# A gated linear recurrence with a SwiGLU feed-forward: rotated rows moved on chip, two units of gates first, feed-forward groups of four chunks

## The chip, the core and the metric

The kernel runs on one core of a Trainium2 chip. TensorE (PE) multiplies matrices, VectorE (DVE) and ScalarE (ACT) work on elements, GpSimd (POOL) does one small operation for each chunk, and SyncE (SP) issues nearly all transfers in the order of its queue. The metric is the device time of one execution in microseconds (us). Every matmul here is in float32, and the profile shows each of them as two instructions.

## The reference

Four sequences of 768 steps, eight heads of 48 features. Each head carries a complex 48 x 48 state that decays and rotates with a gate of its own for each feature and step; the output goes through an RMS norm and a SwiGLU feed-forward of 384 to 1536 to 384.

```python
mag = np.sqrt(a_re * a_re + a_im * a_im)
scale = np.minimum(mag, 0.999) / (mag + 1e-06)
a_re_n, a_im_n = (a_re * scale, a_im * scale)
for t in range(S):
    ar, ai = (a_re_n[:, :, t, :, None], a_im_n[:, :, t, :, None])
    new_re = ar * S_re - ai * S_im
    new_im = ar * S_im + ai * S_re
    kv = np.einsum('bhd,bhe->bhde', k[:, :, t], v[:, :, t])
    S_re, S_im = (new_re + kv, new_im)
    y[:, :, t] = np.einsum('bhd,bhde->bhe', q[:, :, t], S_re)
...
xn = x / np.sqrt(np.mean(x * x, axis=-1, keepdims=True) + 1e-06) * rms_g
g = xn @ w_gate
return ((g * (1.0 / (1.0 + np.exp(-g)))) * (xn @ w_val)) @ w_out
```

## The kernel before

The 3072 rows are cut into 24 chunks of 128 steps (`C`), six to a sequence. Three pieces of work go over them with different steps.

**Gates, by units of two chunks** (`load_gates(u)` and `gates(u)`, 12 units). Features lie on the partitions, 128 at a time in three blocks j, and the 256 steps of the unit on the free axis, so each element-wise instruction is 128 x 768. Magnitudes are multiplied up within a chunk by one scan (tile `p`, L592) and angles are added up by three scans (L612). Then k is divided and q multiplied by the magnitude, and both by the sine and the cosine of the angle. These four products (L501, `rot<-k,y` and so on) go into the tile `rot`, which has a 129th column for the decay of the chunk. For the matmuls, the 96 rows of a head (48 sine and 48 cosine) must lie on the partitions, with the heads on the free axis. `rot` is therefore written to a buffer in device memory (`way`, L629) and read back in the other shape (`kq`, L631), one transfer each way for each chunk. `gates` is a generator; at each `yield` other work is emitted between its parts. Most tiles of it have one buffer: `s`, `w`, `y`, `r`, `p`, and also `k` and `q`, while `re` and `im` have two.

**Attention, by chunks** (`scores(n)` and `finish(n)`). `scores` multiplies k with q for each head (`s_ps`, L721), masks the result (`am`, L723) and transposes k (`kt_ps`, L732, copied by ACT at L733). `finish` of the chunk adds up the state (`state_ps`, L744), makes the output (`y_ps`, L755 and L757), then a chain of small steps: the square and its sum on ACT (L761), `ssq` on DVE (L762), a power on POOL (L765), the scaled copy `xn` on ACT (L767), three transposes on PE (`xT_ps`, L774), and `xT` on DVE (L775).

**Feed-forward, by groups of `GC` = 3 chunks** (`feed_forward(g)`, 8 groups). For each of 12 blocks f of 128 hidden features, six gate and six value matmul instructions run over the 384 columns of the group (L792); ACT makes the silu into `sg` (L795), and DVE multiplies it with the value into `hT`. Then `out_ps` (L803) adds up over the 12 blocks for each chunk, ACT copies it to `ot`, and SP stores it.

The weights come as eight-byte numbers in this launch, so each of 18 pieces is loaded as `raw` (L659) and narrowed to float32 by one instruction of ACT and six of DVE (`narrow`, L671 to L680).

**The order.** The main loop emits, for each n, `scores(n)` and then `finish(n-1)`. After each yield of these, one or two steps of the running feed-forward (`filler`) and one step of the next unit's gates (`ahead`) are emitted. Group g starts after `finish` of its last chunk. What is emitted is not yet the order on the engines: a planner takes the emitted order as a priority, puts an instruction onto its engine's queue as soon as its own cost estimates say that it is ready, and adds the waits. So later work can fill a gap that the planner sees. On the chip each queue then runs in its fixed order, SP's included. When a pool's buffer is taken again, the new tile waits for all readers and writers of the old one.

```python
for n in range(N + 1):
    if n % UC == 0 and n // UC + 1 < NU:
        for _ in ahead:
            pass
        if n // UC + 2 < NU:
            load_gates(n // UC + 2)
        ahead = gates(n // UC + 1)
```

Of the kernel before, what the change touches and what calls it, by code (L numbers as in the profile page):

```python
# [28 lines left out]
P = 128  # L29
# [442 lines left out]
def fast(tc, ctx, qT, kT, v, a_re, a_im, w_gate, w_val, w_out, rms_g, out, H, bad):  # L472
# [10 lines left out]
    GC = 3  # L483
# [6 lines left out]
    assert NCH % GC == 0 and NCH % UC == 0 and DM % P == 0 and D2 <= P and L * ND == D  # L490
# [23 lines left out]
    def load_gates(u):  # L514
# [15 lines left out]
        for n in range(u * UC, (u + 1) * UC):  # L530
            U[n]["v"] = unit.tile([C, H, D], FP32, tag="v", name="v", bufs=4)
            nc.sync.dma_start(out=U[n]["v"].rearrange("t h d -> t (h d)"),
                              in_=v[n * C:(n + 1) * C, :])

    rot = consts.tile([P, 4 * ND, UC, C + 1], FP32, name="rot")
    nc.vector.memset(rot[:, :, :, C:], 0.0)
    load_gates(0)

    zeros = consts.tile([P, T], FP32, name="zeros")
    nc.gpsimd.memset(zeros, 0.0)
# [17 lines left out]
    def gates(u):  # L560
# [4 lines left out]
        s, w, y, r, p = (prep.tile([P, ND, T], FP32, tag=x, name=x)  # L565
                         for x in ("s", "w", "y", "r", "p"))
# [29 lines left out]
        nc.vector.tensor_copy(  # L596
            out=rot[:, 2 * ND:, :, C].rearrange("p (a j) c -> p a j c", j=ND),
            in_=ends[:, u].unsqueeze(1).to_broadcast([P, 2, ND, UC]))
# [12 lines left out]
        for j in range(ND):  # L611
            nc.vector.tensor_tensor_scan(  # L612
                out=re[:, j], data0=im[:, j], data1=zeros, op0=ALU.add, op1=ALU.add,
# [9 lines left out]
        for i, (x, f) in enumerate(((k, y), (k, s), (q, y), (q, s))):  # L623
            tt(rot[:, i * ND:(i + 1) * ND, :, 0:C], by_chunk(x), by_chunk(f))
        yield
        for i in range(UC):
            n = u * UC + i
            way = dram.tile([4 * DM, C + 1], FP32, tag="way", name="way")
            nc.sync.dma_start(out=way.rearrange("(r p) t -> p r t", p=P), in_=rot[:, :, i])  # L629
            to = unit.tile([D2, 2, H, C + 1], FP32, tag="kq", name="kq", bufs=3)  # L630
            nc.sync.dma_start(out=to.rearrange("d x h t -> d x (h t)"),  # L631
                              in_=way.rearrange("(x d h) t -> d x (h t)", x=2, h=H))
            U[n]["k"], U[n]["q"] = to[:, 0, :, 0:C], to[:, 1, :, 0:C]
            U[n]["decay"] = to[:, 1, :, C:]
        yield
# [26 lines left out]
    def narrow(stage, to, raw):  # L662
# [5 lines left out]
        t, g = (stage.tile([P, n], I32, tag=x, name=x, bufs=1) for x in ("t", "g"))  # L668
        as_to = lambda x: x.rearrange("p (c f) -> p c f", f=cols)

        nc.scalar.activation(out=to, in_=as_to(hi.bitcast(FP32)), func=AF.Square)  # L671
        stt(as_to(g.bitcast(FP32)), to, (1.125 * 2.0 ** -15) ** 2, as_to(hi.bitcast(FP32)), ALU.is_ge)

        nc.vector.tensor_scalar(out=t, in0=g, scalar1=3, scalar2=0x3FFFFFFF,
                                op0=ALU.logical_shift_left, op1=ALU.bitwise_and)
        stt(t, g, -2 ** 30, t, ALU.bitwise_and, ALU.bitwise_or)

        nc.vector.tensor_scalar(out=g, in0=t, scalar1=-2 ** 23, scalar2=None, op0=ALU.bitwise_and)
        stt(to, as_to(lo.bitcast(U32)), 2.0 ** -52, as_to(g.bitcast(FP32)), ALU.mult)
# [32 lines left out]
    def scores(n):  # L712
# [3 lines left out]
        am = u["am"] = unit.tile([C, H, C], FP32, tag="am", name="am")  # L716
        hh = H // 2
        for a in range(2):
# [4 lines left out]
            nc.vector.tensor_tensor(out=am[:, a * hh:(a + 1) * hh], in0=ps, op=ALU.mult,  # L723
# [4 lines left out]
        kt = u["kt"] = unit.tile([C, H, D2], FP32, tag="kt", name="kt")  # L728
        for a in range(2):
# [3 lines left out]
            nc.scalar.copy(out=kt[:, a * hh:(a + 1) * hh], in_=ps)  # L733
# [97 lines left out]
    for n in range(N + 1):  # L831
# [11 lines left out]
        if n > 0:  # L843
            run(finish(n - 1), 2)
# [75 lines left out]
```

## Time and profile before

| | before |
|---|---|
| time, median of 3 runs (lowest to highest) | 891.09 us (880.48 to 893.98) |
| the profiled execution: time, span | 884.13 us, 882.3 us |
| mean granted clock of PE | 0.939 |
| busy: PE, PEld (weight loads), DVE, ACT, POOL | 773.3, 530.1, 426.8, 356.2, 23.2 us |
| gate_ps + val_ps matmuls (576 + 576 of 128x384) | 209.4 + 207.7 us |
| out_ps matmuls (576 of 128x384) | 192.8 us |
| chain that ended last: PE, DMA, DVE, ACT | 80%, 10%, 6%, 2% |
| transfers way and kq | 24 each of 774 KB, 8.9 and 5.7 us from issue to landing |
| moved in all | 81.17 MB |

The span runs from the first instruction to the last, and the execution's time lies 1.8 us above it. Mean durations of matmuls overlap, because they are pipelined: the step from one start to the next is what counts. The "chain that ended last" is followed back from the last instruction; its shares say on what the end depended. Waits are read from the engine that waits: "PE s_ps <- DMA kq" is time in which PE stood until a transfer into kq had landed.

### The profile page before, as it was taken

How to read it: one execution, taken by the hardware profiler on the slowest of the kernel's cores; microseconds unless marked ns; L12 is line 12 of the kernel's file. 1: busy time of each engine (PE TensorE's matmuls, PEld its weight loads, DVE VectorE, ACT ScalarE, POOL GpSimd, SP SyncE). 2: the span in 40 equal slices, each digit the busy share in tenths (PEclk: the TensorE clock that was granted, in tenths of full speed). 3: DMA queues.
4: the chain of work that ended last, by engine and by line, in shares of the span. 5: the costliest groups of instructions: out<-in, count | busy, mean ns of one | idle time of the engine just before them, and what ended most of it. 6: DMA issues, size and time to landing. Idle time of an engine off the chain costs nothing.

```text
span 882.3 us, 8797 instructions
## 1 busy us (share of the span) xinstructions
PE 773.3 (88%) x3370; PEld 530.1 (60%) x3370; DVE 426.8 (48%) x654; ACT 356.2 (40%) x520; POOL 23.2 (3%) x42
## 2 busy tenths in 40 slices
PE   0051879888879999999999999999999999999997
PEld 0051857675455566676666667666666767665554
DVE  5978768858978787768785101210121112210110
ACT  6845565643537887676783111111111111110100
POOL 1000000000000000000000000000000000000000
PEclk9995569968989999989999999999999999999999
DMA  8748374852673565482763120112111100000000
GB/s 293 154 110 201 103 169 118 202 138 72 182 186 101 114 154 156 96 189 71 137 162 73 46 63 26 29 45 55 35 29 45 43 21 1 1 9 19 1 1 30
DMA packets 85602, 81.17 MB, mean 92 GB/s; under 512 B 4144, under 2 KB 74800, under 8 KB 85552
## 3 DMA queue, kind: packets, MB, share of 16 engines
q1 hardware_dynamic: 85120, 80.13, 36.3%
q8 instruction: 28, 0.46, 0.2%
q10 hardware_dynamic: 432, 0.39, 0.1%
q14 instruction: 22, 0.18, 0.1%
HBM read 56.77 MB, written 23.74 MB: 91 GB/s over the span
## 4 chain that ended last, share of the span: by engine, by line
PE 80%; DMA 10%; DVE 6%; ACT 2%; issue 1%; SPq 1%; POOL 0%; ACTq 0%; DVEq 0%
PE val_ps L792 20%; PE gate_ps L792 20%; PE out_ps L803 19%; PE s_ps L721 6%; PE y_ps L755 5%; DMA way<-rot 4%; PE y_ps L757 4%; DMA kq<-way 4%; PE state_ps L744 3%; PE kt_ps L732 2%; DVE rot L501 1%; PE xT_ps L774 1%; DMA raw<-in_w_gate_dram 1%; DVE p L592 1%; DVE g L504 1%
## 5 line engine op out<-in xcount | busy, mean ns | idle before, releaser
L792 PE MATMUL gate_ps<-xT,wg 128*128 128x384 f32 x576 | 209.4, 501 | 5.5 <-DVE wg L501 4.8
L792 PE MATMUL val_ps<-xT,wv 128*128 128x384 f32 x576 | 207.7, 497 | 2.2 <-ACT sg L795 2.2
L803 PE MATMUL out_ps<-wo,hT 128*128 128x384 f32 x576 | 192.8, 491 | 0.2
L792 PEld LDWEIGHTS val_ps<-xT,wv 128*128 128x128 f32 x576 | 111.4, 194 | 80.1 <-issue 4.3
L501 DVE TENSOR_TENSOR hT<-val_ps,sg 128x384 f32<-128x384 f32 x96 | 53.3, 555 | 215.8 <-PE val_ps L792 200.4
L792 PEld LDWEIGHTS gate_ps<-xT,wg 128*128 128x128 f32 x576 | 109.0, 196 | 73.7 <-issue 7.9
L803 PEld LDWEIGHTS out_ps<-wo,hT 128*128 128x128 f32 x576 | 108.7, 192 | 71.7 <-issue 1.8
L721 PE MATMUL s_ps<-kq 96*128 96x128 f32 x384 | 57.2, 311 | 77.3 <-DMA kq<-way 77.3
L795 ACT ACTIVATE sg<-gate_ps 128x384 f32<-128x384 f32 x96 | 47.0, 490 | 176.6 <-PE gate_ps L792 176.2
L721 PEld LDWEIGHTS s_ps<-kq 96*128 96x128 f32 x384 | 55.5, 224 | 84.0 <-DMA kq<-way 55.6
L755 PE MATMUL y_ps<-v,am 128*128 128x48 f32 x384 | 76.0, 294 | 0.0
L757 PE MATMUL y_ps<-state,kq 96*128 96x48 f32 x320 | 68.2, 298 | 0.0
L755 PEld LDWEIGHTS y_ps<-v,am 128*128 128x128 f32 x384 | 62.9, 211 | 1.1
L723 DVE TENSOR_TENSOR am<-s_ps,causal 128x512 f32<-128x512 f32 x48 | 32.7, 688 | 51.5 <-PE s_ps L721 51.4
L761 ACT ACTIVATE x<-y_ps 128x384 f32<-128x384 f32 x24 | 11.8, 491 | 110.6 <-PE y_ps L757 101.4
L757 PEld LDWEIGHTS y_ps<-state,kq 96*128 96x128 f32 x320 | 55.1, 215 | 0.3
L808 ACT COPY ot<-out_ps 128x384 f32<-128x384 f32 x24 | 11.4, 475 | 99.3 <-PE out_ps L803 99.3
L765 POOL TENSOR_TENSOR rs<-ssq,mhalf 128x1 f32<-128x1 f32 x24 | 20.8, 867 | 754.7 <-DVE ssq L762 754.7
L733 ACT COPY kt<-kt_ps 128x384 f32<-128x384 f32 x40 | 17.6, 479 | 50.1 <-PE kt_ps L732 50.1
L744 PEld LDWEIGHTS state_ps<-v,kt 128*96 128x96 f32 x320 | 33.0, 179 | 4.4 <-issue 2.4
L744 PE MATMUL state_ps<-v,kt 128*96 128x48 f32 x320 | 32.6, 259 | 0.0
L762 DVE TENSOR_SCALAR ssq<-ssq 128x1 f32<-128x1 f32 x24 | 3.6, 152 | 58.6 <-ACT x L761 58.6
(100 smaller groups left out, 722.6 us busy)
## 6 DMA issues: line engine op xcount, KB each, us to landing
way<-rot SPq DMA_DIRECT2D x24, 774.0 KB, 8.9
kq<-way SPq DMA_DIRECT2D x24, 774.0 KB, 5.7
re<-in_a_re_dram SPq DMA_DIRECT2D x36, 128.0 KB, 2.6
k<-in_k_dram SPq DMA_DIRECT2D x24, 192.0 KB, 2.9
q<-in_q_dram SPq DMA_DIRECT2D x24, 192.0 KB, 3.3
v<-in_v_dram SPq DMA_DIRECT2D x24, 192.0 KB, 2.4
raw<-in_w_gate_dram SPq DMA_DIRECT2D x6, 768.0 KB, 8.2
raw<-in_w_val_dram SPq DMA_DIRECT2D x6, 768.0 KB, 7.0
```

Source lines behind the costliest of these rows:

```text
L501: nc.vector.tensor_tensor(out=o, in0=x, in1=y, op=op)
L721: nc.tensor.matmul(ps[:, h], lhsT=k[:, a * hh + h], rhs=q[:, a * hh + h], start=True, stop=True)
L723: nc.vector.tensor_tensor(out=am[:, a * hh:(a + 1) * hh], in0=ps, op=ALU.mult, in1=causal.unsqueeze(1).to_broadcast([C, hh, C]))
L732: nc.tensor.transpose(ps[:, h], k[:, a * hh + h], ident[0:D2, 0:D2])
L733: nc.scalar.copy(out=kt[:, a * hh:(a + 1) * hh], in_=ps)
L744: nc.tensor.matmul(ps[:, h], lhsT=u["kt"][:, h], rhs=vv[:, h], start=True, stop=True)
L755: nc.tensor.matmul(ps[:, h], lhsT=am[:, h], rhs=vv[:, h], start=True, stop=prev is None)
L757: nc.tensor.matmul(ps[:, h], lhsT=q[:, h], rhs=prev[:, h], start=False, stop=True)
L765: nc.gpsimd.tensor_tensor(out=rs, in0=ssq, in1=mhalf, op=ALU.pow)
L792: nc.tensor.matmul(p_, lhsT=w_[:, d, fs], rhs=xT[:, d], start=d == 0, stop=d == ND - 1)
L795: nc.scalar.activation(out=sg, in_=gp, func=AF.Silu)
L803: nc.tensor.matmul(ps, lhsT=hT[:, f, i * C:(i + 1) * C], rhs=wo[:, f], start=f == 0, stop=f == NF - 1)
```

## The change

- **The way on chip.** `rot`, `way` and `kq` are gone. The four products go into `ks`, `k`, `qs` and `q` themselves (the cosine products in place), and each of their three blocks is moved by one transfer from SBUF to SBUF into the unit's tiles `kr` and `qr`: 12 transfers, each from 128 partitions with a row of 1 KB to 16 partitions with eight such rows. The decays go through memory by themselves (`dec`, 8 bytes for each feature, and two reads into `de`).
- **Order.** At n = 0 all of `gates(1)` is emitted ahead of `scores(0)`; before, it was emitted in steps between the parts of chunks 0 and 1. The first three weight pieces are emitted, and the feed-forward's pool opened, at n = 2 and not at n = 3.
- **Groups of four.** `GC` is 4: six groups, gate and value matmuls over 512 columns, and group 0 starts after `finish(3)`, which follows `scores(4)`.
- **Room for it.** The silu is written straight into `hT` (no `sg`); `am` and `kt` are made of two half tiles (four and two buffers, so `kt` holds one chunk and not two); `v` has three buffers and not four; `ot` has one and not two; `x` shares `xn`; the zeros of the angle scan are one broadcast column; `narrow` works in the weight's own place with one scratch tile in two buffers.

```diff
-    GC = 3
+    GC = 4
...
-            U[n]["v"] = unit.tile([C, H, D], FP32, tag="v", name="v", bufs=4)
+            U[n]["v"] = unit.tile([C, H, D], FP32, tag="v", name="v", bufs=3)
...
-        nc.vector.tensor_copy(
-            out=rot[:, 2 * ND:, :, C].rearrange("p (a j) c -> p a j c", j=ND),
-            in_=ends[:, u].unsqueeze(1).to_broadcast([P, 2, ND, UC]))
+        dec = dram.tile([DM, UC], FP32, tag="dec", name="dec")
+        nc.sync.dma_start(out=dec.rearrange("(j p) c -> p j c", p=P), in_=ends[:, u])
+        de = unit.tile([D2, H, UC], FP32, tag="decay", name="decay", bufs=3)
+        for a in range(2):
+            nc.sync.dma_start(out=de[a * D:(a + 1) * D].rearrange("d h c -> d (h c)"),
+                              in_=dec.rearrange("(d h) c -> d (h c)", h=H))
...
-        for i, (x, f) in enumerate(((k, y), (k, s), (q, y), (q, s))):
-            tt(rot[:, i * ND:(i + 1) * ND, :, 0:C], by_chunk(x), by_chunk(f))
-        yield
+        kq = {n: unit.tile([D2, H, T], FP32, tag=n, name=n) for n in ("kr", "qr")}
+        for to, x, xs in ((kq["kr"], k, ks), (kq["qr"], q, qs)):
+            for a, (o, f) in enumerate(((xs, s), (x, y))):
+                tt(o, x, f)
+                rows = (1 - a) * D
+                for j in range(ND):
+                    nc.sync.dma_start(out=to[rows + j * L:rows + (j + 1) * L], in_=o[:, j])
+            yield
         for i in range(UC):
             n = u * UC + i
-            way = dram.tile([4 * DM, C + 1], FP32, tag="way", name="way")
-            nc.sync.dma_start(out=way.rearrange("(r p) t -> p r t", p=P), in_=rot[:, :, i])
-            to = unit.tile([D2, 2, H, C + 1], FP32, tag="kq", name="kq", bufs=3)
-            nc.sync.dma_start(out=to.rearrange("d x h t -> d x (h t)"),
-                              in_=way.rearrange("(x d h) t -> d x (h t)", x=2, h=H))
-            U[n]["k"], U[n]["q"] = to[:, 0, :, 0:C], to[:, 1, :, 0:C]
-            U[n]["decay"] = to[:, 1, :, C:]
-        yield
+            U[n]["k"], U[n]["q"] = (kq[x][:, :, i * C:(i + 1) * C] for x in ("kr", "qr"))
+            U[n]["decay"] = de[:, :, i:i + 1]
...
+            am.append(unit.tile([C, hh, C], FP32, tag="am", name="am", bufs=4))
...
+            kt.append(unit.tile([C, hh, D2], FP32, tag="kt", name="kt", bufs=2))
...
-            sg = ffn.tile([P, GT], FP32, tag="sg", name="sg")
-            nc.scalar.activation(out=sg, in_=gp, func=AF.Silu)
-            tt(hT[:, f], vp, sg)
+            nc.scalar.activation(out=hT[:, f], in_=gp, func=AF.Silu)
+            tt(hT[:, f], vp, hT[:, f])
...
-            ot = ffn.tile([C, DM], FP32, tag="ot", name="ot")
+            ot = ffn.tile([C, DM], FP32, tag="ot", name="ot", bufs=1)
...
             ahead = gates(n // UC + 1)
+            if n == 0:
+                for _ in ahead:
+                    pass
...
         if n > 0:
             run(finish(n - 1), 2)
+        if n == UC:
+            for _ in range(EARLY):
+                next(pieces)
+            first.close()
+            ffn = ctx.enter_context(tc.tile_pool(name="ffn", bufs=2))
         if n % GC == 0 and n:
             for _ in filler:
                 pass
-            if n == GC:
-                for _ in range(EARLY):
-                    next(pieces)
-                first.close()
-                ffn = ctx.enter_context(tc.tile_pool(name="ffn", bufs=2))
             filler = feed_forward(n // GC - 1, pieces, ffn)
```

## The prediction

> **What bounds the kernel now.** I read the 40 slices first, then the wait table of TensorE (PE) by stretches, then the windows, then the order of time around the stalls.
>
> The slices (digits are tenths; PEclk is the granted clock) show two kernels in one:
>
> ```profile
> PE   0051879888879999999999999999999999999997
> DVE  5978768858978787768785101210121112210110
> PEclk9995569968989999989999999999999999999999
> ```
>
> From slice 13 on PE is full at full clock while VectorE (DVE) goes idle; before, DVE is 70 to 90% busy and PE has holes and a half clock. Windows, with columns length, busy PE, PEld, DVE, ACT, POOL, clock, DMA share, GB/s:
>
> ```profile
> 49.00:123.00 74.00, 43.56 (x234) 42.34 (x234) 53.49 (x81) 38.84 (x53) 4.08 (x3) 0.61 0.53 135
> 123.00:275.00 152.00, 128.34 (x565) 89.75 (x566) 124.94 (x185) 78.86 (x108) 4.53 (x5) 0.88 0.58 145
> ...
> 400.00:780.00 380.00, 380.00 (x1753) 259.06 (x1752) 112.69 (x191) 98.88 (x173) 7.94 (x13) 1.00 0.21 51
> ```
>
> PE's waits, asked for 0 to 275 us and for the rest: the rest is empty, and the first stretch has
>
> ```profile
> PE s_ps L721 <- DMA kq<-way: 77.3, 5, 48.8
> PE xT_ps L774 <- ACT xn L767: 15.4, 6, 6.4
> PE gate_ps L792 <- DVE wg L501: 4.8, 2, 3.1
> ```
>
> So the time is: when PE becomes saturated, plus the PE work that is left then. Group 0 of the feed-forward starts at 122.9 and ends at 275.1; what follows is 882.3 - 275.1 = 607.2 us without a wait of PE. From PE's order of time:
>
> ```profile
> 86.02 3.75 PE L721 MATMUL s_ps<-kq 96*128 96x128 f32 x16 [17.28 <-DMA kq<-way]
> ...
> 122.94 3.82 PE L792 MATMUL gate_ps<-xT,wg 128*128 128x384 f32 x6 [0.65 <-DVE xT L775]
> ...
> 275.11 2.10 PE L792 MATMUL gate_ps<-xT,wg 128*128 128x384 f32 x6
> 277.05 2.10 PE L792 MATMUL val_ps<-xT,wv 128*128 128x384 f32 x6
> ```
>
> **Part 1, groups of four.** At full clock six gate matmuls of 384 columns start 1.935 us apart from the next six, so 0.3225 us each. 128-column ones (s_ps, 16 in 1.78 us) take 0.111, so a line through both gives 0.428 for 512 columns; plain proportion gives 0.430. A group of three costs 24 x 1.935 + 23.2 (72 out_ps, from 852.96 on) = 69.7 us; one of four 24 x 2.58 + 96 x 0.3225 = 92.9. Eight groups of the one are 557.6, six of the other 557.4: the PE work itself is not shortened. What changes is what is behind PE when it saturates. At the end of group 0, four chunks instead of three are through, 23.2 us more. With the same chunks 0 to 7 and chunk 8's scores done, the rest is 607.2 - 23.2 = 584.0.
>
> Group 0 is also where the weights are narrowed. One piece costs DVE 4 x 0.87 + 2 x 0.47 = 4.4 us (start to start), a pair of gate and value pieces 8.8, and the hT products of its two f-steps 0.9. PE streams those two steps in 7.7 us now and in 10.3 after: six pairs in which PE outran DVE by 2.0 us become six in which it doesn't. That is 12 us of loss.
>
> The silu written into hT saves no instruction and adds no wait: hT is freed by the last out_ps, which precedes gate_ps on PE's queue anyway. ACT and DVE get fewer, longer instructions (96 x 0.56 to 72 x about 0.7 us), hidden by PE's 2.6 us per accumulation. One ot buffer: its copy comes every 7.7 us, its store lands in 1.8. All 0; without that cover 24 x 1.8 us at most.
>
> **Part 2, two units first.** Today unit 1's products end on DVE at 70.5. Between 36.1 and 70.5, DVE waits 3.4 + 0.9 + 0.7 us for s_ps and state_ps of chunks 0 and 1, and does four masks and a state, 2.9 us. Put behind unit 1's gates, these 7.9 leave the way: 62.6. Bounds: 0 to 16 (another 8 us of narrowing lies there, which only fills gaps). If the gap filling already does all that, it is 0.
>
> **Part 3, the way on chip.** The chain that ended last shows the hop through memory, and SP's order of time the price of an issue with 1 KB rows:
>
> ```profile
> 34.88 7.19 DMA way<-rot
> 42.08 6.66 DMA kq<-way
> 48.79 3.78 PE s_ps L721 x16
> ```
> ```profile
> 27.24 1.83 SPq L522 DMA_DIRECT2D re<-in_a_re_dram  x3
> ```
>
> and the page's table of issues its landing (KB each, median us from issue):
>
> ```profile
> re<-in_a_re_dram SPq DMA_DIRECT2D x36, 128.0 KB, 2.6
> ```
>
> Removed per unit: two way and two kq transfers, 14.2 us from the last product (34.6) to s_ps (48.8). Added: 12 transfers of 128 KB from SBUF to SBUF, plus dec and two de. The nearest row is re: 128 KB in 128 rows of 1 KB, 0.61 us to issue, 2.6 to land. The first three can go when the first product is done, 2.6 us before the last: 12 x 0.61 + 2.6 - 2.6 = 7.3 us after the last product, a gain of 6.9. Bounds: 4.1 (all 1.57 MB at the 232 GB/s that the two kq made in 6.66 us, 6.7 - 2.6), and 12 x 2.6 - 2.6 = 28.6 (each waits for the one before it). I take 7.3, since re's issues do go out back to back. The four products stay (0.95 us each); two small copies give way to dec and de, whose small rows I price at gcol's 5.4 us each; they leave some ten DVE instructions before the products, so they are hidden, else up to 10.8 us.
>
> Against this speaks the Trainium skill, "SBUF — State Buffer", section "Door 1: The DMA port swizzle": a transfer reaches only the ports of its partitions, and partitions 0 to 15 get 104 GB/s. Each of these transfers writes 16 partitions; an estimate from that page is 1.26 us each and 15 us for twelve, so about 15 after the last product in place of 7.3, and a sum some 8 to 15 us longer. No row here has so few partitions.
>
> **New waits.** k and q are now read by transfers, in one buffer: the load of the next unit's k must wait for them, and behind it on SP's queue stand the later loads, v, and weight pieces; DVE waits for k in mid-gates. k's rows leave about 5 us after unit 0's products, the load lands 3 us later, and q follows 4 us on; in unit 1 q*p runs at 58.0, 23 us after those products. Covered; if not, 5 us a unit for units 1 to 4. v has three buffers: v of chunk n waits for y of n-3, a place where SP already stood 72 us before 275 with way(2) behind it (products done at 111.8, way issued at 119.0). I leave that as it is: 0, at most 7. SP's issues per unit go from 16 to 27, some 15 us of a 50 us unit. kt has two halves, so its copies wait for the state matmuls of the chunk before; these need only masks, 0 to 1 us.
>
> **The sum.** Unit 1 arrives at 62.6 + 7.3 = 69.9, not 86.0. From there PE does scores(2), finish(1), scores(3), finish(2), as now in 122.3 - 86.0 = 36.3 us, and then, new, scores(4) (5.0 at half clock) and finish(3) (13.8, as from 108.5 to 122.3) before group 0 may start: 125.0. Unit 2 is there by then (products near 100, arrival near 107). The group's stretch holds, at full clock, 92.9 plus the attention of chunks 4 to 8 (5.2 + 5.7 + 5.9 + 7.7 + 2.4 = 26.9): 119.8. Today's stretch holds 104 in 152.2: 48 lost, half of it waits, half low clock after them. Of these I take away the 12 of part 1 and half of the 22 that kq's 11.2 us of waits and the slow matmuls behind them cost: 25 remain (bounds 10 and 48). Saturated at 125.0 + 119.8 + 25 = 269.8; plus 584.0 = 853.8. The execution lies 1.8 us above its span (884.1 to 882.3): 855.6. The median of the runs is 0.8% above that execution, so I say 857.
>
> **Rivals.**
> 1. The stall stays. The order on each queue is fixed beforehand, so PE may wait behind the wrong instruction as before, and the full 48 us remain: 857 + 23 = 880, no change. For it: half of the 48 are short waits in other places. Against: the six pairs are a plain balance of DVE and PE.
> 2. The boundary opens. A group has 12 + 2 x 4 = 20 steps, four chunks call 22 to 24, so the last finish of a group has no matmuls to cover y to xT, 3.4 us today (117.8 to 121.4). Five boundaries x (3.4 + as much again at half clock) = 34 at most: 891. For it: after a 3.1 us wait at 181.2, 16 s_ps took 3.75 us, not 1.95. Against: the next chunk's scores, of a unit already there, can stand in. The skill's "TensorE: Matmul & The Clock Gate" (section "Why this matters for your kernels") says that idle gaps over about 3 us bring the half clock; by it four or five boundaries would all cost that.
> 3. Slower: a ring of loads and transfers. If the twelve run one after the other, X us a unit, then k and q of the next unit load only X later and its gates end about 11 after that: unit 0 arrives at 32 + X, unit 2 another 2(X + 11) later, at 54 + 3X, and group 0 starts 19 after it, at 73 + 3X. At X = 31 (12 x 2.6) that is 166, 41 late: 857 + 41 = 898. In the first 86 us the DMA engines are 70 to 80% busy, and kq then took up to 8.9 us where its median is 5.7; by that factor X is 48, the start 217 and the time 949. I price the rival at its middle, X = 40: 193, 68 late, 925. It decides against the change from X = 28 (2.3 us a transfer), where the start at 157 eats the whole gain. For it: one SP queue, one buffer. Against: re's issues overlap.
> 4. The new order does nothing, because gaps were filled with unit 1 anyway (its first DVE instruction is at 36.1 already): 8 us less, 865.
>
> **How the numbers follow.** Forecast 0.44, rival 1 0.14, 2 0.12, 3 0.20, 4 0.10. A measurement of this kernel tells about 2% from no change: under 873 is faster, over 909 slower. Forecast and 4 are faster but for 0.03, and 1 and 2 give 0.04 more: 0.55. Slower is 0.13 of rival 3 (X over 35) and 0.07 for the waits that I set to 0, if several come together: 0.20. The rest, 0.25, is within. The likeliest's own range is 842 to 872; the range for 8 in 10 goes from 832 (loss 10 us, as if each hole but a few closed) to 915 (X = 37), with 0.05 left out below and 0.15 above.
>
> **What would show it.** Unit 1's s_ps near 70 and not 86; a kr or qr transfer under 3 us to landing, twelve issued in some 8 us; group 0's first gate_ps of 512 columns at about 125 and its last out_ps at about 270; gate_ps at 2.58 us per six; DVE waits for s_ps before 70 gone; PE without waits after 270. I am wrong if SP stands at k's load while DVE waits for it, if PE waits for xn at the end of each group, or if gate_ps has waits on wg and wv as long as now.

## The result, and the profile after

The changed kernel is slower: 926.83 us (923.8 to 933.6) against 889.24 us for the kernel before in the same comparison, a ratio of 1.047 [1.036, 1.058]. The forecast was 857 us, with a range from 832 to 915. The profiled execution after has a span of 923.8 us (before: 882.3). Some executions of one and the same kernel come out over 1.5% slower than its fastest; the ratios here and below are taken over the others, so a ratio need not be that of the two medians beside it.

The slices of the page after, on the scale of those shown before:

```profile
PE   0024665897978999999999999999999999999997
DVE  5998446667999765637147352174211121101100
PEclk9996555797889899999999988999998999899999
```

PE becomes full about one slice later, and its half clock (the 5s of PEclk) lasts longer. VectorE (DVE), which stood mostly at 6 to 8 in the fifth to the ninth slice, is at 4 to 6 there. Neither engine is full there: PE waits in turn for a mask of DVE, for transfers and for ACT. The windows (length, busy PE, PEld, DVE, ACT, POOL, clock, DMA share, GB/s), cut at the start and at the end of group 0:

```profile
45.00:170.60 125.60, 63.92 (x324) 61.50 (x325) 83.39 (x115) 63.12 (x85) 3.54 (x4) 0.63 0.39 73
170.60:322.00 151.40, 135.40 (x487) 79.10 (x486) 122.95 (x164) 71.89 (x96) 5.96 (x4) 0.88 0.45 116
322.00:923.00 601.00, 593.69 (x2275) 348.43 (x2274) 196.52 (x295) 186.93 (x279) 10.72 (x16) 0.97 0.21 44
```

Of the 70.0 us between the sum (853.8) and the span, 45.6 are the late start of group 0 (170.6 instead of 125.0), 6.4 its stretch (to 321.8: 151.2 instead of 144.8), and 18 the rest (602 instead of 584). PE's order of time has the stations that the sum went by:

```profile
51.86 3.76 PE L721 MATMUL s_ps<-qr,kr 96*128 96x128 f32 x16 [51.86 <-DMA k<-in_k_dram]
...
70.41 3.78 PE L721 MATMUL s_ps<-qr,kr 96*128 96x128 f32 x16 [13.52 <-DVE am L724]
...
95.90 3.75 PE L721 MATMUL s_ps<-qr,kr 96*128 96x128 f32 x16 [12.59 <-DMA qr<-q]
...
144.72 3.76 PE L721 MATMUL s_ps<-qr,kr 96*128 96x128 f32 x16 [10.28 <-DMA re<-in_a_re_dram]
...
170.62 2.74 PE L793 MATMUL gate_ps<-xT,wg 128*128 128x512 f32 x6
```

These are the scores of chunks 0, 1, 2 and 4, and the first gate matmuls. (The waits at 51.86 and 144.72 are put down to loads of `k` and `re`, but the last `qr` of units 0 and 2 lands at 51.5 and 144.5, just before.) Unit 1's scores come at 95.9 (before 86.0, forecast 69.9), unit 2's at 144.7. SP's order of time shows what stood in front of unit 1's and unit 2's transfers:

```profile
71.25 1.26 SPq L628 DMA_DIRECT2D kr<-ks  x2
80.27 0.36 SPq L532 DMA_DIRECT2D v<-in_v_dram  x1
80.67 0.56 SPq L628 DMA_DIRECT2D kr<-ks  x1
81.36 1.85 SPq L628 DMA_DIRECT2D kr<-k  x3
83.72 0.56 SPq L628 DMA_DIRECT2D qr<-qs  x1
87.59 0.94 SPq L526 DMA_DIRECT2D k<-in_k_dram  x2
88.58 1.19 SPq L628 DMA_DIRECT2D qr<-qs  x2
89.82 1.91 SPq L628 DMA_DIRECT2D qr<-q  x3
...
181.61 0.59 SPq L657 DMA_DIRECT2D raw<-in_w_val_dram  x1
```

Unit 1's last product on DVE ends at 75.3. Its third `kr` transfer and all that follow stand behind a load of v that waits for the output of chunk 0 (80.3), and the last five stand also behind the load of unit 2's k, which waits until `kr<-k` has been read (87.6). The last line is the sixth weight piece: before, it was issued at 84.57.

```profile
84.57 0.41 SPq L659 DMA_DIRECT2D raw<-in_w_val_dram  x1
```

### The profile page after: what moved, and what is told of

The parts are those of the page before. It is cut to its first block, busy times and chain, and to the rows that moved or that the text cites. A ratio compares the mean times of both kernels' runs of the same rounds, so it can differ in the third digit from the quotient of the medians.

```text
span 923.8 us, 8331 instructions
## 1 busy us (share of the span) xinstructions
PE 793.0 (86%) x3082; PEld 489.0 (53%) x3082; DVE 437.5 (47%) x617; ACT 352.7 (38%) x495; POOL 22.4 (2%) x42
## 4 chain that ended last, share of the span: by engine, by line
PE 76%; DVE 10%; ACT 3%; issue 2%; POOL 1%; DMA 1%; DVEq 0%; ACTq 0%; SPq 0%; POOLq 0%
PE out_ps L803 20%; PE val_ps L793 18%; PE gate_ps L793 18%; PE y_ps L757 5%; PE y_ps L759 5%; PE s_ps L721 4%; PE state_ps L746 3%; PE kt_ps L733 1%; PE xT_ps L775 1%; DVE t L504 1%; DVE wo L504 1%; DVE wv L504 1%; POOL rs L767 1%; DVE t L674 1%; DVE im L504 1%
## 5 line engine op out<-in xcount | busy, mean ns | idle before, releaser
L793 PE MATMUL val_ps<-xT,wv 128*128 128x512 f32 x432 | 202.1, 604 | 8.7 <-DVE wv L501 8.7
L793 PE MATMUL gate_ps<-xT,wg 128*128 128x512 f32 x432 | 204.3, 610 | 2.1 <-DVE wg L501 2.1
L501 DVE TENSOR_TENSOR hT<-val_ps,hT 128x512 f32<-128x512 f32 x72 | 49.7, 691 | 217.6 <-PE val_ps L793 214.4
L793 PEld LDWEIGHTS val_ps<-xT,wv 128*128 128x128 f32 x432 | 83.5, 194 | 115.2 <-issue 102.0
L721 PE MATMUL s_ps<-qr,kr 96*128 96x128 f32 x384 | 60.4, 324 | 88.2 <-DMA k<-in_k_dram 51.9
L793 PEld LDWEIGHTS gate_ps<-xT,wg 128*128 128x128 f32 x432 | 81.5, 196 | 91.3 <-issue 88.7
L795 ACT ACTIVATE hT<-gate_ps 128x512 f32<-128x512 f32 x72 | 43.0, 597 | 209.4 <-PE gate_ps L793 208.9
L721 PEld LDWEIGHTS s_ps<-qr,kr 96*128 96x128 f32 x384 | 58.8, 238 | 94.6 <-issue 79.7
L759 PE MATMUL y_ps<-state,qr 96*128 96x48 f32 x320 | 70.0, 304 | 0.0
L759 PEld LDWEIGHTS y_ps<-state,qr 96*128 96x128 f32 x320 | 56.7, 221 | 0.0
L746 PEld LDWEIGHTS state_ps<-v,kt 128*96 128x96 f32 x320 | 33.7, 182 | 15.4 <-DVE am L724 8.8
L776 DVE TENSOR_TENSOR xT<-xT_ps,gcol 128x384 f32<-128x384 f32 x24 | 13.3, 554 | 48.5 <-PE xT_ps L775 48.5
```

What stands on the lines that cost most here:

```text
L501: nc.vector.tensor_tensor(out=o, in0=x, in1=y, op=op)
L721: nc.tensor.matmul(ps[:, h], lhsT=k[:, a * hh + h], rhs=q[:, a * hh + h], start=True, stop=True)
L746: nc.tensor.matmul(ps[:, h], lhsT=u["kt"][h * 2 // H][:, h % (H // 2)], rhs=vv[:, h], start=True, stop=True)
L759: nc.tensor.matmul(ps[:, h], lhsT=q[:, h], rhs=prev[:, h], start=False, stop=True)
L776: nc.vector.tensor_tensor(out=G[g]["xT"][:, :, i * C:(i + 1) * C], in0=ps, op=ALU.mult, in1=gcol.unsqueeze(2).to_broadcast([P, ND, C]))
L793: nc.tensor.matmul(p_, lhsT=w_[:, d, fs], rhs=xT[:, d], start=d == 0, stop=d == ND - 1)
```

## The experiments

All ratios are against the kernel before, run on the same chip beside it; where nothing else is said, the medians are of four executions.

### Which part costs it

Four parts were undone one at a time, and one was done alone.

Groups of three again:

```diff
-    GC = 4
+    GC = 3
```

> The changed kernel with groups of three chunks again, all else as changed. Three theories stand: Q, that the 12 transfers of a unit stand on SP's queue behind v loads that wait for y and behind k loads, so units 1 and 2 arrive late; D, that DVE is late (gates of unit 1 and weight pieces ahead of the masks, and the two tensor_scalar of a piece take 0.94 us in place of 0.55); G, that group 0 of four starts late only because it needs finish(3), which stands behind scores(4). G expects group 0 to start after finish(2), near 135 in place of 170.6, and nearly all of the loss back: 890 to 900. Q and D expect the earlier start too, but 23 us less work in group 0 and the same late units 2 and 3, so 905 to 920.

922.67 us, 1.041 [1.030, 1.052]. Group 0 starts at 131.5 instead of 170.6, but takes until 290.4, with 19.6 us of waits for narrowed `wv` and 10.2 for `wo`. Groups of four are not the cost.

The old order of units 0 and 1:

```diff
-            if n == 0:
-                for _ in ahead:
-                    pass
```

> The changed kernel without the emission of all gates(1) ahead of scores(0). Q: the masks of chunk 0 come back in front (first one at 69.7 now, 51 before the change), y(0) ends some 12 us earlier, so does the v load that waits for it, and unit 1's kr transfers leave SP without that wait: unit 1's s_ps at about 85 in place of 95.9, time 910 to 918. D: the same masks, but DVE's total is unchanged: 918 to 926. G: 926, no difference.

926.35 us, 1.035 [1.021, 1.050]; group 0 from 169.6 to 320.8. The order of emission makes no difference that shows.

Four buffers for v (and one for the scratch tile of `narrow`, to make room):

```diff
-            U[n]["v"] = unit.tile([C, H, D], FP32, tag="v", name="v", bufs=3)
+            U[n]["v"] = unit.tile([C, H, D], FP32, tag="v", name="v", bufs=4)
...
-        t = stage.tile([P, n], I32, tag="t", name="t")
+        t = stage.tile([P, n], I32, tag="t", name="t", bufs=1)
```

> The changed kernel with four buffers for v again (room from one buffer in place of two for the scratch tile t, which only DVE touches). Q: v loads wait for the y of a chunk further back, the transfers of units 1 to 3 leave SP earlier: unit 1's s_ps near 86 in place of 95.9, unit 2's near 125 in place of 144.7, group 0 at 150 in place of 170.6, time 903 to 912. D and G: within 5 us of 927.

932.95 us, 1.051 [1.041, 1.060]. SP stands at v as before (to 83.3, 116.3 and 134.0): it is now the load for one chunk later, in the same place of the queue.

The way through memory put back, all else as changed:

```diff
-        kq = {n: unit.tile([D2, H, T], FP32, tag=n, name=n) for n in ("kr", "qr")}
...
+            way = dram.tile([4 * DM, C + 1], FP32, tag="way", name="way")
+            nc.sync.dma_start(out=way.rearrange("(r p) t -> p r t", p=P), in_=rot[:, :, i])
```

> The changed kernel with the way through device memory again (rot, way, kq and the decays in their 129th column), all else as changed: two transfers for each chunk, and k and q free as soon as DVE has read them. Q: only two issues for each chunk stand behind v loads, and the k load waits for no transfer: group 0 starts near 140, time 895 to 905, that is 20 to 30 us less than the change. D: 920 to 930. G: 930 or a little more, since the way takes 14 us and not 7.

898.42 us, 1.010 [0.998, 1.023]. The on-chip way is the cost: without it, what is left of the change can't be told from no change. The converse, the on-chip way alone in the kernel before (with the silu in hT, for room):

```diff
-            sg = ffn.tile([P, GT], FP32, tag="sg", name="sg")
-            nc.scalar.activation(out=sg, in_=gp, func=AF.Silu)
-            tt(hT[:, f], vp, sg)
+            nc.scalar.activation(out=hT[:, f], in_=gp, func=AF.Silu)
+            tt(hT[:, f], vp, hT[:, f])
...
+        kq = {n: unit.tile([D2, H, T], FP32, tag=n, name=n) for n in ("kr", "qr")}
```

> The kernel before with the way on chip alone (12 transfers, dec and de), and the silu written into hT to make room; groups of three, four buffers for v, gates(1) in steps. Q: the transfers themselves put unit 1 and 2 behind v loads; group 0 starts near 132 in place of 122.9, unit 2 and 3 come late within it, time 900 to 912, that is slower than before by 1 to 2%. If the cost lies in the combination with the order and the groups, 885 to 893, no change.

915.59 us, 1.037 [1.023, 1.052]. Both directions agree.

### Which wait carries it

The loads of v issued by POOL, in the changed kernel:

```diff
-            nc.sync.dma_start(out=U[n]["v"].rearrange("t h d -> t (h d)"),
+            (nc.gpsimd if u else nc.sync).dma_start(out=U[n]["v"].rearrange("t h d -> t (h d)"),
```

> The changed kernel with the loads of v issued by POOL from unit 1 on; nothing else moves, and the order on PE is the same up to group 0. Four buffers for v did not help, since SP still stood at a v load until y of an earlier chunk was done (83.3, 116.3 and 134.0 us). Q, now as a chain: y(1) and y(2) end, then SP passes the v load, then the rest of unit 2's transfers go, then scores(4), finish(3) and group 0. With v off SP, unit 1's transfers leave when DVE has made the products (s_ps near 88 in place of 95.9), unit 2's too (s_ps near 128 in place of 144.7), group 0 starts near 152 in place of 170.6, time 903 to 913. If the transfers or DVE are what is late in themselves, nothing moves: 922 to 930.

918.11 us, 1.036 [1.025, 1.047]: perhaps 9 us, and the intervals overlap. Unit 1's scores come at 90.0 and unit 2's at 129.9, yet group 0 starts only at 166.4.

`narrow` as before, with two scratch tiles:

```diff
-        stt(to, to, (1.125 * 2.0 ** -15) ** 2, hf, ALU.is_ge)
+        stt(as_to(g.bitcast(FP32)), to, (1.125 * 2.0 ** -15) ** 2, as_to(hi.bitcast(FP32)), ALU.is_ge)
```

> The changed kernel with the narrowing of the weights as before (scratch tiles t and g, contiguous, so the two tensor_scalar of a piece take 0.55 us and not 0.94). D: DVE gets 18 x 0.8 = 14 us back, all before the end of group 0; the chain to group 0 shortens by some 4 to 8 us where pieces stand in it, group 0's waits on wv, wg and wo (13 us) shrink: time 912 to 920. Q: the pieces are beside the chain, 920 to 926.

933.22 us (919 to 935), no gain that shows.

`finish(3)` and group 0 emitted ahead of `scores(4)`:

```diff
+        if n == GC:
+            run(finish(n - 1), 2)
+            filler = feed_forward(0, pieces, ffn)
             run(scores(n), 1)
```

> The changed kernel with finish(3) and group 0 emitted ahead of scores(4), so that group 0 needs units 0 and 1 only. G: group 0 starts at about 148 in place of 170.6 (scores(3) at 117, finish(2), finish(3)), PE works on it while unit 2 is on its way, time 900 to 910. Q alone: the same start, but units 2 and 3 are as late as now and PE stands within group 0 instead: 912 to 922.

932.85 us, 1.050 [1.035, 1.065]. Group 0 starts 22 us earlier, at 148.1, and ends later, at 324.6. PE now waits 36.4 us for narrowed weights, 17.7 of it at one place (waits of PE between 148 and 325 us, with columns us, times, longest):

```profile
PE gate_ps L793 <- DVE wg L501: 20.1, 3, 17.7
PE out_ps L803 <- DVE wo L501: 10.1, 5, 2.8
PE val_ps L793 <- DVE wv L501: 6.2, 1, 6.2
```

This was the first sign that the start of group 0 isn't what sets its end.

The kernel before with the decays alone by `dec`:

```diff
+        dec = dram.tile([DM, UC], FP32, tag="dec", name="dec")
...
-            U[n]["decay"] = to[:, 1, :, C:]
+            U[n]["decay"] = de[:, :, i:i + 1]
```

> The kernel before, k and q by way and kq as there, with only the decays carried by dec and two reads for each unit (and the silu written into hT). Doing the whole on-chip way in the kernel before cost 3.7%. If SP's stand at dec (65.8 us in the changed kernel) makes a large part of that, this run is at 900 to 910; if the 12 transfers alone make it, 886 to 896.

890.48 us, 0.999 [0.995, 1.003], of ten executions: free. SP stands 44.7 us at `dec` in this run, and that costs nothing; the 65.8 us of the changed kernel were not tried by themselves.

### Transfers or order

The 12 transfers issued by POOL:

```diff
-                    nc.sync.dma_start(out=to[rows + j * L:rows + (j + 1) * L], in_=o[:, j])
+                    nc.gpsimd.dma_start(out=to[rows + j * L:rows + (j + 1) * L], in_=o[:, j])
```

> The changed kernel with its 12 transfers a unit issued by POOL; v and dec stay on SP. Theory of the queue: the transfers cost time because on SP they stand among loads of v, k and q that wait; then s_ps(4) comes 15 to 25 us before its 144.7 and the time falls to 895 to 908. Theory of the order: the planner lays VectorE's masks of chunk 0 behind unit 1's k*r whoever issues the transfers; then the first mask still runs at 65 to 70, s_ps(4) comes at 130 to 145, and the time stays 915 to 930.

932.44 us, 1.052 [1.043, 1.060]. The scores of chunk 1 now wait 32.9 us for chunk 0's mask, and group 0 starts at 203.1. POOL's queue is no remedy, and the loss takes another path there: PE has no wait for weights at all, but 54.5 us of waits for `xn` up to 330 us (15.4 before).

All transfers kept, in the old order of emission, and DVE's order forced by holding later work behind the masks:

```diff
+            if count[0] in {3: 0, 4: 1}:
+                with tc.issue_after(masks[{3: 0, 4: 1}[count[0]]]):
+                    next(ahead, None)
...
+                    with tc.issue_after(masks[i - 1]):
+                        next(pieces)
```

> The changed kernel with all its transfers, emitted in the old order (unit 1's gates in steps between the parts of chunks 0 and 1), and with one thing forced: on VectorE the masks of chunks 0 and 1 stand ahead of the second half of unit 1's gates and of the second and third weight piece. Theory of the order: the masks run as soon as the scores are there, at 53 to 62 us (69.7 to 75 in the changed kernel), y of chunk 0 ends near 66 instead of 80, the scores of unit 2 come at 120 to 132 instead of 144.7, group 0 starts at 150 to 160, and the time is 900 to 915. Theory of the transfers: they cost their time on SP and in traffic whatever VectorE does; group 0 starts at 165 or later and the time stays 920 to 932.

922.74 us, 1.044 [1.037, 1.052]. The masks did move, from 69.7 to 52.2:

```profile
52.15 0.69 DVE L725 TENSOR_TENSOR am<-s_ps,causal 128x512 f32<-128x512 f32 x1 [2.72 <-PE s_ps L722]
```

Unit 2's scores then come at 142.7 instead of 144.7. SP stands before them as before (v at 115.6 and 128.7, each with transfers of unit 2 behind it), and group 0 runs from 166.9 to 317.5. So the late masks carry little of the loss. With v on POOL as well:

```diff
-            nc.sync.dma_start(out=U[n]["v"].rearrange("t h d -> t (h d)"),
+            (nc.gpsimd if u else nc.sync).dma_start(out=U[n]["v"].rearrange("t h d -> t (h d)"),
```

> As a_order, and the loads of v issued by POOL. v off SP alone gave 9 us (918). If both waits are separate, the time is 890 to 905 and unit 2's scores come at 110 to 125; if they are the same wait seen twice, it stays within 5 us of a_order.

915.55 us, 1.031 [1.024, 1.038]; group 0 from 171.3 to 317.9. Not the 890 to 905 of two separate waits.

Now the transfers alone. In the kernel before, 12 a unit from `rot` into a spare tile that nobody reads:

```diff
+        for m in range(2):
+            to = unit.tile([D2, H, UC, C], FP32, tag="spare", name="spare", bufs=1)
+            for a in range(2):
+                for j in range(ND):
+                    r = (1 - a) * D + j * L
+                    nc.sync.dma_start(out=to[r:r + L], in_=rot[:, (2 * m + 1 - a) * ND + j, :, 0:C])
```

> The kernel before with its way through memory, and 12 transfers of 128 KB more for each unit from rot into a spare tile that nobody reads (rows of two times 512 bytes instead of 1 KB; to make room, v has three buffers, ot one, x shares xn, the silu goes into hT, the zeros are one column). They stand on SP's queue among the way's transfers, and the masks of chunk 0 stand behind unit 1's k*r on VectorE's queue, as in the changed kernel. If the transfers' issues (12 x 0.62 us) and the order that comes with them are the cost, the time is 910 to 930; if only a reader that waits for such transfers pays, 888 to 900.

917.62 us, 1.036 [1.031, 1.040], of five. Nobody uses their data, and they cost what the whole on-chip way costs. (SP also waits for the one spare tile to come free, 15.4 us up to 330 us and 30.9 in all.) The sixth weight piece is issued at 155.5, and PE waits for weights (waits of PE up to 330 us):

```profile
PE val_ps L797 <- DVE wv L501: 15.8, 4, 6.9
PE out_ps L807 <- DVE wo L501: 13.9, 4, 7.3
```

The same bytes in two transfers a unit, 128 partitions to 128:

```diff
+            to = unit.tile([P, 2 * ND, UC, C], FP32, tag="spare", name="spare", bufs=1)
+            nc.sync.dma_start(out=to, in_=rot[:, 2 * m * ND:2 * (m + 1) * ND, :, 0:C])
```

> As b_extra (the kernel before, with transfers from rot that nobody reads), but the 1.57 MB of a unit go in two transfers of 768 KB, 128 partitions to 128, in place of twelve of 128 KB into 16 partitions. If the number of the transfers on SP's queue is what costs, the time is 888 to 900; if their bytes, it stays at 910 to 920 as in b_extra (917.6).

892.29 us, 1.000 [0.994, 1.006], of ten. All other edits of the run before are in this one too. So it is not the bytes or the changes that make room, but the number of transfers, or their 16 partitions; these two were not separated. And the twelve issued by POOL:

```diff
-                    nc.sync.dma_start(out=to[r:r + L], in_=rot[:, (2 * m + 1 - a) * ND + j, :, 0:C])
+                    nc.gpsimd.dma_start(out=to[r:r + L], in_=rot[:, (2 * m + 1 - a) * ND + j, :, 0:C])
```

> As b_extra, twelve transfers a unit that nobody reads, but issued by POOL, which does only the small power of each chunk beside them. VectorE's queue has the masks of chunks 0 and 1 at the same places as in the kernel before. If place and order on the queues cost the 28 us of b_extra, the time is 888 to 900; if the chip's traffic into 16 partitions costs them, whoever issues, it is 908 to 920 with the first masks as early as before (51 to 58 us).

918.08 us, 1.028 [1.018, 1.037]. The cost is there off SP too, but in another place: the sixth weight piece goes at 81.4 and group 0 ends at 277.9, 2.6 after that of the kernel before, but it starts at 162.7, and the outputs of chunks 6 and 7, done by then in the kernel before, still have to come. Up to 330 us PE waits 41.4 us for `xn` there, and not at all for weights. The transfers take 6.8 us to land there (4.3 from SP), and `way` 11.6 (9.5). Whether those slower landings or POOL's own queue cost the 25 us was not separated.

### What is left without the transfers

The changed kernel with the way through memory, as above, and v on POOL:

```diff
+            way = dram.tile([4 * DM, C + 1], FP32, tag="way", name="way")
...
+            (nc.gpsimd if u else nc.sync).dma_start(out=U[n]["v"].rearrange("t h d -> t (h d)"),
```

> The changed kernel with the way through memory put back (as in the run without the transfers, 898 us, first gate_ps at 165) and with the loads of v issued by POOL. There SP stood at v(3) and v(4) to 106.8 and 124.4 us, and unit 2's k, q and way were queued behind it (way issued at 126.9, s_ps(4) at 143.7). Theory: v's wait for the output of the chunk three before is what holds unit 2; off SP, its way goes at 100 to 110, group 0 starts at 145 or earlier, and the time is 870 to 888. Rival: unit 2 is held by the planned order of VectorE; group 0 still starts at 160 to 166 and the time is 893 to 900.

890.36 us, 0.9995 [0.995, 1.004], of ten; group 0 from 149.6 to 279.5. The kernel before, with v on POOL alone:

```diff
-            nc.sync.dma_start(out=U[n]["v"].rearrange("t h d -> t (h d)"),
+            (nc.gpsimd if u else nc.sync).dma_start(out=U[n]["v"].rearrange("t h d -> t (h d)"),
```

> The kernel before with the loads of v issued by POOL, nothing else. Before 275 us SP stood 72 us at v there, but the loads of gates behind it were needed only later. If v's place on SP's queue costs the old kernel something, it is the 7 us by which way(2) went late (products done at 111.8, issued at 119.0): 880 to 886. If it costs nothing, 887 to 894, as the 0 of the prediction has it.

890.84 us, 1.003 [0.998, 1.008], of ten; group 0 from 118.3 to 267.6. And the first of these with `narrow` as before, and `finish(3)` and group 0 ahead of `scores(4)`:

```diff
+        t, g = (stage.tile([P, n], I32, tag=x, name=x, bufs=1) for x in ("t", "g"))
...
+            run(finish(n - 1), 2)
+            filler = feed_forward(0, pieces, ffn)
             run(scores(n), 1)
```

> The changed kernel with the way through memory put back, v issued by POOL, the weights narrowed with the two scratch tiles of before, and finish(3) and group 0 emitted ahead of scores(4). With the first two of these alone it was 890, group 0 from 149.6 to 279.5. If the start of group 0 decides, it starts at 125 to 132, ends at 262 to 270, and the time is 872 to 884. If VectorE's work decides (it was busy 230 of the first 280 us there), group 0 starts as early, waits for narrowed weights, ends at 274 to 280, and the time is 885 to 895.

884.83 us, 0.999 [0.995, 1.002], of ten. Group 0 starts at 129.5, 20 us earlier than in the first of the three, and ends at 285.4, 6 later, with one more chunk's output done by then. No version was measurably better than the kernel before.

### One table over the runs

Read from SP's order of time (the sixth weight piece), from DVE's instructions on `wo` (start of the last `wo<-t,wo`), and from PE's order of time (group 0). Times in us.

| run | small transfers issued by | sixth weight piece issued | last piece narrowed | group 0 | time |
|---|---|---|---|---|---|
| before | none | 84.6 | 270.1 | 122.9 to 275.3 | 889 |
| before, v on POOL | none | 88.6 | 262.5 | 118.3 to 267.6 | 891 |
| before, two large ones | none | 75.7 | 265.3 | 128.8 to 274.7 | 892 |
| change, way by memory, v on POOL | none | 88.2 | 262.6 | 149.6 to 279.5 | 890 |
| ... and group 0 first, old `narrow` | none | 89.8 | 275.1 | 129.5 to 285.4 | 885 |
| change, way by memory | none | 91.4 | 282.0 | 165.0 to 301.9 | 898 |
| before, on-chip way | SP | 142.7 | 279.6 | 130.6 to 286.4 | 916 |
| before, twelve unread | SP | 155.5 | 286.7 | 126.5 to 291.8 | 918 |
| change, groups of three | SP | 144.2 | 282.6 | 131.5 to 290.4 | 923 |
| change, v on POOL | SP | 153.0 | 299.8 | 166.4 to 311.2 | 918 |
| change, masks forced | SP | 178.4 | 307.3 | 166.9 to 317.5 | 923 |
| change | SP | 181.6 | 308.6 | 170.6 to 321.8 | 927 |
| change, group 0 first | SP | 158.9 | 314.5 | 148.1 to 324.6 | 933 |
| before, twelve unread by POOL | POOL | 81.4 | 272.1 | 162.7 to 277.9 | 918 |
| change, the twelve by POOL | POOL | 64.2 | 235.1 | 203.1 to 321.4 | 932 |

Two things stand out. In all rows but the last, group 0 ends 5 to 20 us after the last weight piece is narrowed, wherever it starts between 118 and 171. And the sixth weight piece is issued at 76 to 92 without the small transfers and at 143 to 182 with them on SP; the runs left out of the table lie at 89 (decays alone) and at 158 to 185 (transfers on SP), and none between.

The first is partly built in: group 0 emits most of these pieces itself, and its last `out_ps` needs the last of `wo`. Nor are the ends of equal worth: by then PE has made the outputs (`y_ps`) of chunks 0 to 7 in the kernel before and in the changed one, but only of 0 to 6 in the rows "before, on-chip way", "before, twelve unread", "groups of three" and "change, group 0 first". And the last row shows the loss without late weights. What speaks for the weights where SP issues the transfers are PE's waits for narrowed weights: 4.8 us before, 31.5 with the twelve unread (span 28.1 us longer), 26.9 with the on-chip way alone (26.2 longer), 36.4 with group 0 first. In the changed kernel itself they are 13.1; there most of what the sum missed is the late start.

In the changed kernel all five pieces loaded at the start were narrowed by 68.9 (the `wg<-t,wg` at 67.93), so from there to 181.6 DVE had no piece to fill its gaps with, and it was busy 53.4 of the 95 us from 75 to 170:

```profile
67.93 0.96 DVE L501 TENSOR_TENSOR wg<-t,wg 128x768 f32<-128x768 f32 x1
68.81 0.95 DVE L501 TENSOR_TENSOR k<-k,r 128x768 f32<-128x768 f32 x1
69.68 0.68 DVE L724 TENSOR_TENSOR am<-s_ps,causal 128x512 f32<-128x512 f32 x1
```

That the twelve small transfers cost 3 to 4% is shown, from both sides. That late weight pieces are how they cost it on SP is argued from these waits and the order of the queue, not shown: weight loads on a queue of their own, with the transfers kept, were not tried, and on POOL the loss comes without them.

## Why the prediction was wrong, step by step

**The step that failed: the start of group 0 as the start of saturation, with the new waits on SP put at 0.** The sum was start + content + a loss, with the weights in the loss. The start came at 170.6 and not at 125.0. Of these 45.6 us, 12.7 are unit 1's last product on DVE (75.3 instead of 62.6), 13.3 are its way to PE (20.6 us to 95.9, instead of 7.3, with ten of the twelve transfers behind the loads of v and k on SP), and 19.6 are what follows up to group 0. The prediction had these waits in view ("0, at most 7", "covered; if not, 5 us a unit") and had counted SP's issues (16 to 27 a unit, "some 15 us of a 50 us unit"), and put them at nothing. These are the terms that were mis-sized.

Nor was the start the bound that the sum took it for. Started 22 us earlier in the changed kernel, group 0 ended 3 us later, with one chunk's output less done; started 20 us earlier without the transfers, it ended 6 us later, with one more done. Where SP issues the transfers, its end lies behind the last narrowed weight piece. The prediction did see that DVE and PE are close to balance there, and priced it as 12 us to be gained by longer groups; it named the weight pieces among what stands behind k's load on SP, but gave that no price. How much of the loss each of the two carries, the late units and the late weights, stays open.

**Part 3, 7.3 us after the last product.** Unit 0: the last product ends at 38.7, the scores start at 51.9: 13.2 us, and 10.4 (36.3 to 46.7) with the on-chip way alone, against 14.2 before. So 1 to 4 us were gained in unit 0, not 6.9; in unit 1, by which the sum goes, the way took 20.6 us, longer than before. The twelve issues do take 7.8 us as forecast (36.1 to 43.9). What fails is "under 3 us to landing". The page after has medians of 3.5 and 4.2, and the tile `qr` in unit 0, issued last, more:

```profile
kr<-ks SPq DMA_DIRECT2D x36, 128.0 KB, 3.5
kr<-k SPq DMA_DIRECT2D x36, 128.0 KB, 4.2
```
```profile
DMA to landing us min/median/max: 6.0/7.3/8.2
```

They pile up: 1.57 MB from the first issue to the last landing in 12.4 us (34.1 to 46.5, on-chip way alone) and 15.4 us (36.1 to 51.5, changed kernel). In the changed kernel the issues are some 0.65 us apart and the landings some 1.1. The Trainium skill, "SBUF — State Buffer", section "Door 1: The DMA port swizzle", has 104 GB/s for partitions 0 to 15, from which the prediction estimated 15 us for the twelve. The second row lies at this estimate and the first below it, though other transfers ran beside them. The prediction weighed that rule and went by the row of `re`, which has 128 partitions: the nearest row in size, not in shape.

**Part 2, 7.9 us.** Unit 1's products end at 75.3, not at 62.6. Unit 0's already end 4 us later than before (38.7, not 34.7), and between the two DVE was not idle: from 36 to 75 it has 19 instructions on weights; before, from 36 to 70.5, it had 9. Ten more at 0.87 us from start to start are an estimated 8.7 us, which uses up the gain. The prediction had the work in view ("another 8 us of narrowing lies there, which only fills gaps") but let it only leave the gap, not enter a new one. The outcome is that of rival 4, with weights as the filling.

**From unit 1's scores to group 0, 55.1 us forecast.** It took 74.7 (95.9 to 170.6): unit 2's scores came at 144.7 and not by 107, and the scores of chunk 5, which the sum had inside the group, came ahead of it, 3.1 us. The waits for v and for k are both there on SP, and each holds back transfers of the unit behind it. Taken away one by one they give little: off SP, v gives at most some 9 us, and four buffers give nothing.

**Part 1, groups of four.** The work of PE is as computed: six gate matmuls of 512 columns start 2.58 us apart, and without the transfers group 0 takes 130 us with four chunks (149.6 to 279.5) where it took 152 with three. That is less than the 145 forecast, partly because the scores of chunk 5 are done before it, and it is given back by the later start.

**Rest, 584 us.** It took 602. A granted clock of 0.97 in place of 0.99 is an estimated 12 of the 18 (602 x 0.02); the other 6 are unassigned (the scores of chunk 8 are done before group 0 ends in both kernels). Rival 2 did not come: after 322 us PE waits once, 2.2 us.

**Rival 3** priced 925 and the time was 927, but mostly by chance. Its sign, place (one SP queue, one buffer) and start (193, in fact 170.6) were near; its mechanism, 2.6 to 4 us for each transfer after the other, was not: unit 0's land 1.1 us apart, and the long time of unit 1's comes from the loads in front of them. By its formula 170.6 is X = 32.5 us, and the time would have been 857 + 45.6 = 903. It left out the weight pieces behind the ring. (The forecast itself has a slip: 0.8% on 855.6 is 862, not 857.)

**Signs.** Held: DVE's waits for `s_ps` before 70 are gone (because the mask is late), and 2.58 us per six. Failed: unit 1's scores, the landing, the start and the end of group 0. Of the signs of being wrong, SP does stand at k's load (20.6 us for `kr<-k`, 21.9 at q's for `qr<-q`), though DVE hardly waits for k (2.1 us): what stands behind it on SP pays. PE's waits on `wg` and `wv`, 4.8 us before, are 10.7 after, so that sign of being wrong came too.

## What to carry to other kernels

When a change turns a few large transfers into many small ones on an in-order queue, count not only their own time but what comes after them on that queue, the low-priority loads above all: here the next unit's transfers stood behind loads that waited, and so, most likely to some cost, did the weight pieces that the next stage needs. Before shortening the way to a stage's start, look at what its end follows across versions; a start that comes 20 us earlier while the end doesn't isn't the bound. And price a transfer by the row that has its shape (partitions written), not only its bytes.

## What the hardware showed that was not expected

**Three blocks in place of one row: tensor_scalar takes 0.94 us, not 0.55.** `narrow` in the weight's own place reads or writes a slice of the weight. DVE's groups by shape, after:

```profile
L678 DVE TENSOR_SCALAR wv<-t 128x768 int32<-128x768 int32 x6 | 5.7, 949 | 0.0
...
L678 DVE TENSOR_SCALAR wo<-t 128x768 int32<-128x768 int32 x6 | 3.4, 561 | 0.0
```

Before, all were 549 ns. `wg` and `wv` have three blocks of 256 columns in a piece, `wo` two of 384 in a row. The Trainium skill, "VectorE: DVE Perf Modes", section "What auto-detection actually checks", asks, for the mode in which an instruction with one source takes two elements a cycle, for outermost dimensions that are both even or equal in source and destination; three blocks against one contiguous row is neither. The times agree with it, though no run changes the number of blocks alone. 24 instructions by 0.395 us are 9.5 us of DVE, which the prediction did not have. A pair of gate and value pieces then costs DVE an estimated 12 x 0.87 + 0.9 = 11.3 us, more than PE's 10.3 for its two f-steps, so the balance behind Part 1's 12 us was gone; undone alone (the run with the old `narrow`), the slower instructions gave no gain that shows.

**The half clock came without a gap.** After 322 us there are a few spells of it, as this one from PE's order of time:

```profile
569.31 0.39 PE L759 MATMUL y_ps<-state,qr 96*128 96x48 f32 x2
569.53 0.50 PE L757 MATMUL y_ps<-v,am 128*128 128x48 f32 x2
569.83 0.63 PE L759 MATMUL y_ps<-state,qr 96*128 96x48 f32 x2
...
573.48 0.90 PE L775 MATMUL xT_ps<-ident,xn 128*128 128x128 f32 x3 [2.17 <-ACT xn L768]
574.18 3.62 PE L721 MATMUL s_ps<-qr,kr 96*128 96x128 f32 x16
```

PE has no wait in the record from 322 us up to this one, and the pairs of 48-column matmuls go from 0.39 to 0.63 us at 569.5, ahead of the 2.2 us wait (granted clock 0.50 from 569.7 to 577). The Trainium skill's "TensorE: Matmul & The Clock Gate" (section "Why this matters for your kernels") has idle gaps over about 3 us as the cause; here no such gap came before it, only matmuls back to back. Why is open.
